# A fast-matmul MLP kernel on one core: every steady step issued from one list, row half by row half, with the side strip's matmuls kept among the main ones

## The chip, the cores and the metric

One core of a Trainium2 chip. The time is device microseconds of one launch. A profile of one execution comes beside it: what each engine (TensorE PE and its weight loader PEld, VectorE DVE, ScalarE ACT, GpSimd POOL, SyncE SP) did and when.

## What is computed

Two blocks in a row, all in fp32: a light convolution over 7 positions with weights softmaxed per head (8 heads, 192 channels, 8 sequences of 4096), then an MLP with a sigmoid GELU (192 to 2048 to 192).

```python
w = np.exp(weight - weight.max(-1, keepdims=True)); w /= w.sum(-1, keepdims=True) + 1e-9
x_pad = np.concatenate([np.zeros((B, 6, D)), x], axis=1)
conv[b, s, h, :] = sum(w[h, k] * x_pad[b, s + k, h, :] for k in range(7))
h = conv.reshape(B * S, D) @ moe_w_in            # (32768, 192) @ (192, 2048)
g = h * (1.0 / (1.0 + np.exp(-1.702 * h)))
out = g @ moe_w_out                              # (32768, 2048) @ (2048, 192)
```

## The kernel before

Both matmuls are done by a fast scheme in blocks: sums of blocks of the inputs and of the weights are multiplied, and the products are added up again, so that fewer products are needed. The work is cut into 32 steps (`N_BIG`), each of 512 tokens from each half of the batch. Step 0 and most of step 1 are the opening, which also prepares the weights; step 31 is the last. A step has two stages on TensorE.

**First stage (products).** For each of two halves `v` of the hidden dimension there are 20 products (`TERMS`). `product1` (L598) issues one as two matmuls, for the row halves h0 and h1: 64 x 128 weights, 512 columns, one in the upper 64 rows of the array and one in the lower, so that two run at a time. The results gather in four pairs of PSUM banks, `slot0` to `slot3` (`sums` is the last); `slot20` is bank pair 2 for h0, `slot21` the same for h1. A product on top of an earlier one in its bank waits until whoever reads the earlier one has done so: DVE adds and subtracts them (`sum2`, L639), ACT copies them out to SBUF rooms (`copy2`, L633, with its sign turned L635), ACT's GELUs read PSUM by halves (L615) or a room at once (L620). The names in the lists: `a0` to `a8` are bank pairs, `k0` to `k10` places in the rooms, and two k names may share one room (k8 and k4 do). POOL meanwhile adds the convolution's taps for the next step (L501, 12 additions a step) and sums of its blocks (`vsum`, L355 and L357), SP copies these sums to the other row half (`cross`, L526); DVE makes the first sums of GELU blocks ("early g", five of them, one by an accumulating DMA on POOL's queue, L831: `(8, 0, "acc")`, spot 8 gets spot 0 added).

**Second stage.** 20 forms times sums of GELU blocks go to PSUM as 78 main steps, each of three matmuls of 128 x 32 weights and 256 columns in the column strips 0, 1 and 2 of the array (L855), and seven more forms go as 78 side matmuls to strip 3 (also L855). DVE makes the sums of GELU blocks just ahead (`sum`, 128 x 1024), adds up the results (`join`), and transposes them (`turn`, L771); ACT copies side results out (L880) and seeds banks (L884), and computes taps of later steps (L483); SP stores (L782).

**What sets the order.** All engines take their instructions in the order in which the program lists them. For the first stage that is `ORDER` (line 646 on), whose items always issue both row halves, h0 and then h1; for the second stage `PLAN` (790 on). There a `("go", n)` issues n times one main step and the next side matmul, so the sequence is always main c0, c1, c2, side. What is done for later steps comes from queues (`next_tap`, `next_add`, `next_sum`, `cross_piece`): a list's item says only that the next one of its queue is issued here. The last step uses the same lists, with what belongs to later steps left out.

The banks of the second stage are the three that come free, in the order in which they come free: `bx`, `bs`, `by`. Mains write their h0 banks in the order `bs, bx, by` and the sides write the h1 banks, `sides = (bx[1], bs[1], by[1])`: a column of the form goes to the first, the next to the second, and so on.

```python
def go(n):
    for _ in range(n):
        w, t = now["steps"].pop(0)
        for c in range(NC):
            one_matmul(chunk(now["to"], c), w[:, chunk_cols(c)], t, now["first"], not now["steps"])
        now["first"] = False
        d, ws, ts, st, to = side.pop(0)
        one_matmul(d, ws, ts, st, to is not False)
```

## Time and profile before

| what | value |
| --- | --- |
| median of 3 runs | 2262.71 us (2261.76 to 2263.1) |
| the profiled execution | 2262.78 us, its span 2261.1 us |
| granted TensorE clock | 1.00 |
| a steady step, first stage / second stage | 35.42 / 33.94 us |
| the last step | 35.07 / 33.88 us |
| end of the last matmul to the end of the span | 2255.57 to 2261.1 us |

The span is what the profile covers; the execution's own time is 1.7 us more. Lines with "chain" come from the profile's way back from the last instruction: at each step to what released it. In a row of the timeline stand start, duration, engine, line, operation, output and input by the program's names, shapes, the number of instructions in the row and, in brackets, the idle time before it with what ended it. An fp32 matmul leaves two records on PE and two weight loads on PEld.

### The profile page before, as it was taken

Reading aid. Unit: us, or ns where it says so; the run is one execution under the profiler, and the core shown is the slowest. Engines: PE = TensorE matmul, PEld = TensorE weight load, DVE = VectorE, ACT = ScalarE, POOL = GpSimd, SP = SyncE. Lnnn points to the kernel's source line nnn. Section 1 sums busy time; section 2 is a strip of 40 time slices with the busy share of each in tenths; the row PEclk is TensorE's granted clock in tenths of the full one; section 3 lists DMA queues with packets and bytes.
Section 4 is the critical chain, followed back from the end, with each engine's and each line's share of the span. In section 5 each row is a group of like instructions: output and inputs, shape, how many; then the busy total and the mean of one; then the engine's idle time right before and its main releaser. Section 6 shows DMA issues by size and latency. Waiting matters only on the chain.

```text
span 2261.1 us, 62136 instructions
## 1 busy us (share of the span) xinstructions
PE 2248.2 (99%) x24966; PEld 1552.0 (69%) x24966; DVE 1985.3 (88%) x2970; ACT 1707.7 (76%) x3233; POOL 1063.9 (47%) x1098
## 2 busy tenths in 40 slices
PE   9999999999999999999999999999999999999999
PEld 5366567766777766777667776667776677766775
DVE  8998888988889888889888898888988888988888
ACT  8677877777777778777787777787777877777754
POOL 1545544455543555444555445554355544455510
PEclk9999999999999999999999999999999999999999
DMA  8986657766667666576565776666866657765543
GB/s 198 174 158 133 125 114 150 143 128 127 121 131 159 128 128 126 111 160 140 125 132 114 141 152 128 129 124 118 163 134 128 124 114 151 144 127 103 104 92 71
DMA packets 275679, 298.05 MB, mean 132 GB/s; under 512 B 119104, under 2 KB 203328, under 8 KB 275392
## 3 DMA queue, kind: packets, MB, share of 16 engines
q0 software_dynamic: 57648, 150.69, 37.0%
q1 hardware_dynamic: 216096, 142.99, 27.8%
q8 instruction: 198, 3.24, 0.6%
q14 instruction: 89, 0.73, 0.1%
q10 hardware_dynamic: 1648, 0.39, 0.1%
HBM read 53.15 MB, written 25.17 MB: 35 GB/s over the span
## 4 chain that ended last, share of the span: by engine, by line
PE 96%; DVE 2%; ACT 1%; issue 1%; DMA 1%; POOL 0%; DVEq 0%; ACTq 0%; POOLq 0%; SPq 0%
PE slot L598 49%; PE slot L855 45%; PE slot L1120 1%; DVE g L357 1%; DMA g<-osbs 0%; PE slot L1115 0%; DVE room L357 0%; ACT g L615 0%; PE slot L946 0%; DVE room L639 0%; ACT w_form L483 0%; DMA xin<-in_x_dram 0%; DVE slot L639 0%; DVE room L355 0%; DVE osbs L771 0%
## 5 line engine op out<-in xcount | busy, mean ns | idle before, releaser
L598 PE MATMUL slot<-conv_t,w_in_s 64*128 64x512 f32 x5152 | 1147.4, 594 | 3.3 <-ACT room L633 1.5
L598 PEld LDWEIGHTS slot<-conv_t,w_in_s 64*128 64x128 f32 x5152 | 663.3, 186 | 474.6 <-issue 312.1
L855 PE MATMUL slot<-g,w_form 128*32 128x256 f32 x9672 | 894.2, 379 | 0.7 <-DVE room L357 0.7
L855 PEld LDWEIGHTS slot<-g,w_form 128*32 128x32 f32 x9672 | 575.6, 110 | 128.9 <-DVE room L357 2.1
L501 POOL TENSOR_TENSOR conv_t<-conv_t,g 128x512 f32<-128x512 f32 x354 | 449.0, 1275 | 88.4 <-ACT g L483 65.4
L855 PE MATMUL slot<-g,w_out_s 128*32 128x256 f32 x5952 | 467.5, 379 | 1.3 <-DVE g L357 0.8
L357 DVE TENSOR_TENSOR g<-g 128x1024 f32<-128x1024 f32 x372 | 450.4, 1224 | 8.0 <-DMA g<-osbs 1.0
L880 ACT COPY room<-slot 32x256 f32<-32x256 f32 x651 | 237.2, 364 | 289.8 <-PE slot L855 281.5
L639 DVE TENSOR_TENSOR room<-slot,room 128x512 f32<-128x512 f32 x620 | 383.6, 679 | 67.8 <-PE slot L598 67.8
L633 ACT COPY room<-slot 128x512 f32<-128x512 f32 x620 | 337.7, 595 | 77.7 <-PE slot L598 61.7
L483 ACT ACTIVATE g<-xt,cw 128x512 f32<-128x512 f32 x534 | 353.9, 715 | 3.7
L620 ACT ACTIVATE g<-room 128x1024 f32<-128x1024 f32 x248 | 265.7, 1071 | 79.0 <-DVE room L639 49.3
L615 ACT ACTIVATE g<-slot 128x512 f32<-128x512 f32 x528 | 282.5, 610 | 51.9 <-PE slot L598 32.8
L831 POOL DMA_DIRECT2D g<-g x124 | 128.1, 1038 | 355.0 <-PE slot L855 330.8
L639 DVE TENSOR_TENSOR slot<-slot,room 128x512 f32<-128x512 f32 x372 | 239.7, 689 | 53.8 <-PE slot L598 52.2
L855 PEld LDWEIGHTS slot<-g,w_out_s 128*32 128x32 f32 x5952 | 239.7, 110 | 43.2 <-DVE room L639 23.3
L355 POOL TENSOR_TENSOR conv_t<-conv_t 128x256 f32<-128x256 f32 x210 | 179.3, 860 | 129.2 <-PE slot L598 119.6
L855 PE MATMUL slot<-osbs,w_form 128*32 128x256 f32 x2232 | 229.5, 379 | 0.0
L506 POOL DMA_DIRECT2D g<-g x120 | 105.9, 883 | 238.1 <-ACT g L483 99.4
L855 PEld LDWEIGHTS slot<-osbs,w_form 128*32 128x32 f32 x2232 | 132.5, 110 | 23.6
L639 DVE TENSOR_TENSOR slot<-room,slot 128x512 f32<-128x512 f32 x124 | 79.8, 687 | 41.8 <-PE slot L598 41.8
L855 PE MATMUL slot<-room,w_form 128*32 128x256 f32 x1488 | 112.9, 379 | 0.0
(166 smaller groups left out, 1662.6 us busy)
## 6 DMA issues: line engine op xcount, KB each, us to landing
g<-g POOLq DMA_DIRECT2D x124, 512.0 KB, 6.5
xin<-in_x_dram SPq DMA_DIRECT2D x240, 180.0 KB, 4.2
conv_t<-conv_t SPq DMA_DIRECT2D x186, 192.0 KB, 5.4
g<-g POOLq DMA_DIRECT2D x120, 256.0 KB, 5.4
conv_t<-conv_t SPq DMA_DIRECT2D x186, 128.0 KB, 2.9
out_dram<-osbs SPq DMA_DIRECT2D x186, 128.0 KB, 2.7
g<-room POOLq DMA_DIRECT2D x31, 512.0 KB, 5.1
conv_t<-g POOLq DMA_DIRECT2D x60, 256.0 KB, 5.4
```

The costliest lines, as they stand in the source:

```text
L355: eng.tensor_add(v(dst), v(a), v(b))
L357: eng.tensor_sub(v(dst), v(a), v(b))
L483: act.mul(home, conv_src(big, c, k), cw[:, c, k : k + 1])
L501: nc.gpsimd.tensor_add(dst, dst, home)
L598: nc.tensor.matmul(slot[h], w_in_s[halves[h], a, v * P : (v + 1) * P], src, start=first, stop=True, skip_group_check=True,)
L615: act.activation(dst[:, :, h, :], src[h].rearrange("p (o t) -> p o t", o=2), AF.Gelu_apprx_sigmoid, scale=float(sign),)
L620: act.activation(dst.rearrange("p o h t -> p h o t"), src.rearrange("p h (o t) -> p h o t", o=2), AF.Gelu_apprx_sigmoid, scale=float(sign),)
L633: act.copy(bank(dst, h), bank(src, h))
L639: op(*(bank(t, h) for t in (dst, a, b)))
L831: nc.gpsimd.dma_start(out=spot(dst), in_=spot(a), accum_op=ALU.add)
L855: nc.tensor.matmul(dst, w, t, start=first, stop=last, skip_group_check=True)
L880: act.copy(to, d)
```

## The change

The two lists and the queues are replaced by one list, `STEP` (L543 on), that names every instruction of a steady step (steps 2 to 30) one by one: products, sums, copies and GELUs of a single row half, a main step `("m", i)`, a side matmul `("s", i)`, each tap, tap addition, sum and crossing copy by its own number. The last step has a list of its own, `LAST` (L1161 on). The opening is written out in the same way. The multiset of instructions on each engine stays as it was; one store of the last step moves from ACT's DMA queue to SP's.

```diff
-    ORDER = [
-        (0, "prod", 6, "a8"), (0, "sum", "k0", "a8", "-", "k8"), (0, "prod", 2, "a3"), (0, "copy", "k4", "a3", 1),
...
-    PLAN = [
-        ("side", 13, 16, "k0"), ("main", 1, 5, "p2", 1), ("vsum",), ("go", 2), ("sum", 14, 14, "-", 18), ("go", 1),
...
+    STEP = [
+        ("add", 1, 2, 5), ("tap", 1, 1, 6), ("add", 1, 1, 6), ("prod", 0, 6, "a8", 0),
+        ("sum", 0, "k0", "a8", "-", "k8", 0), ("prod", 0, 6, "a8", 1), ("sum", 0, "k0", "a8", "-", "k8", 1),
...
+        ("begin", 0), ("s", 0), ("s", 1), ("m", 0), ("m", 1), ("s", 4), ("m", 3), ("s", 7), ("m", 5),
...
+        ("s", 68), ("turn", 0, 0, 1, "k1"), ("turn", 0, 1, 1, "k2"), ("t", 20), ("m", 74),
...
-        mains, sides = (bs[0], bx[0], by[0]), (bx[1], bs[1], by[1])
+        mains, sides = (bs[0], bx[0], by[0]), (by[1], bx[1], bs[1])
...
+    def main_part(i):
+        dst, w, t, first, last = now["todo"][i]
+        for c in range(NC):
+            one_matmul(chunk(dst, c), w[:, chunk_cols(c)], t, first, last)
+
+    def side_part(i):
+        d, w, t, first, to = now["aside"][i]
+        one_matmul(d, w, t, first, to is not False)
...
+    opening()
+    for big in range(2, N_BIG - 1):
+        run(STEP, big)
...
+    run(LAST, N_BIG - 1)
```

Products are now issued by L483, second-stage matmuls by L744, copies and seeds by L537, turned copies by L539, GELUs by L500, side copies by L779, taps by L446, tap additions by L450, accumulating DMAs by L533, sums and joins by L343 and L345. In the second stage two or three sides, or two or three main steps, may now follow each other directly; counted along the list, the number of sides issued is at no point more than two ahead of the main steps, nor more than one behind.

**Start of a steady step's first stage.** PE, before: the products 6, 2, 12, 16 and 14, whole.

```order
L598 MATMUL slot00_67<-conv_t_78,w_in_s_79 128x512
L598 MATMUL slot01_68<-conv_t_78,w_in_s_79 128x512
L598 MATMUL slot20_71<-conv_t_78,w_in_s_79 128x512
L598 MATMUL slot21_72<-conv_t_78,w_in_s_79 128x512
L598 MATMUL slot30_73<-conv_t_78,w_in_s_79 128x512
L598 MATMUL slot31_74<-conv_t_78,w_in_s_79 128x512
L598 MATMUL slot10_69<-conv_t_78,w_in_s_79 128x512
L598 MATMUL slot11_70<-conv_t_78,w_in_s_79 128x512
```

PE, after, at the same place: 6 (both halves), 12 of h0, 2 of h1, 12 of h1, 2 of h0, 16 of h1 and of h0.

```order
L483 MATMUL slot00_67<-conv_t_78,w_in_s_79 128x512
L483 MATMUL slot01_68<-conv_t_78,w_in_s_79 128x512
L483 MATMUL slot30_73<-conv_t_78,w_in_s_79 128x512
L483 MATMUL slot21_72<-conv_t_78,w_in_s_79 128x512
L483 MATMUL slot31_74<-conv_t_78,w_in_s_79 128x512
L483 MATMUL slot20_71<-conv_t_78,w_in_s_79 128x512
L483 MATMUL slot11_70<-conv_t_78,w_in_s_79 128x512
L483 MATMUL slot10_69<-conv_t_78,w_in_s_79 128x512
```

Products 2 and 12 have changed places in h0 only. Then come 9 of h0 and 14 of h1; before, 14 of h0 and h1, and 9 behind it. ACT's first copies, before, behind the last side copy of the step before:

```order
L880 COPY room_76<-slot11_70 32x256
L483 ACTIVATE g_75<-xt_2189,cw_143 128x512 x3
L633 COPY room_76<-slot20_71 128x512
L633 COPY room_76<-slot21_72 128x512
L483 ACTIVATE g_75<-xt_2189,cw_143 128x512
L633 COPY room_76<-slot10_69 128x512
L633 COPY room_76<-slot11_70 128x512
```

and after:

```order
L779 COPY room_76<-slot11_70 32x256
L446 ACTIVATE g_75<-xt_2186,cw_143 128x512 x3
L537 COPY room_76<-slot21_72 128x512
L537 COPY room_76<-slot20_71 128x512
L537 COPY room_76<-slot10_69 128x512
L537 COPY room_76<-slot11_70 128x512
```

The copy of product 2 into k4 takes h1 first, and no tap stands between it and the copy of product 16 into k1.

**Start of the second stage.** PE, before: the last product, and main steps and sides in turn (a row x3 is one main step, a row with an h1 slot one side).

```order
L598 MATMUL slot31_74<-conv_t_78,w_in_s_79 128x512
L855 MATMUL slot00_67<-g_75,w_out_s_80 32x256 x3
L855 MATMUL slot01_68<-g_75,w_form_81 32x256
L855 MATMUL slot00_67<-g_75,w_out_s_80 32x256 x3
L855 MATMUL slot01_68<-g_75,w_form_81 32x256
```

PE, after:

```order
L483 MATMUL slot30_73<-conv_t_78,w_in_s_79 128x512
L744 MATMUL slot11_70<-g_75,w_form_81 32x256 x2
L744 MATMUL slot00_67<-g_75,w_out_s_80 32x256 x6
L744 MATMUL slot01_68<-g_75,w_form_81 32x256
L744 MATMUL slot00_67<-g_75,w_out_s_80 32x256 x3
L744 MATMUL slot01_68<-g_75,w_form_81 32x256
L744 MATMUL slot00_67<-g_75,w_form_81 32x256 x6
```

Two sides come first, in another bank (slot11, the tile whose last reader is a GELU, instead of slot01, which a DVE sum reads last), then two main steps in a row.

**POOL ahead of the second stage.** Before, from the run of tap additions (L501) on; L831 is the accumulating DMA into spot 8:

```order
L501 TENSOR_TENSOR conv_t_78<-conv_t_78,g_75 128x512 x12
L355 TENSOR_TENSOR conv_t_78<-conv_t_78 128x256
L357 TENSOR_TENSOR conv_t_78<-conv_t_78 128x256
L355 TENSOR_TENSOR conv_t_78<-conv_t_78 128x256
L357 TENSOR_TENSOR conv_t_78<-conv_t_78 128x256
L355 TENSOR_TENSOR conv_t_78<-conv_t_78 128x256 x3
L831 DMA g_75<-osbs_77 128x1024
L357 TENSOR_TENSOR conv_t_78<-conv_t_78 128x256 x2
L355 TENSOR_TENSOR conv_t_78<-conv_t_78 128x256 x2
```

After:

```order
L450 TENSOR_TENSOR conv_t_78<-conv_t_78,g_75 128x512 x11
L343 TENSOR_TENSOR conv_t_78<-conv_t_78 128x256
L345 TENSOR_TENSOR conv_t_78<-conv_t_78 128x256
L450 TENSOR_TENSOR conv_t_78<-conv_t_78,g_75 128x512
L343 TENSOR_TENSOR conv_t_78<-conv_t_78 128x256
L345 TENSOR_TENSOR conv_t_78<-conv_t_78 128x256
L343 TENSOR_TENSOR conv_t_78<-conv_t_78 128x256 x3
L345 TENSOR_TENSOR conv_t_78<-conv_t_78 128x256
L343 TENSOR_TENSOR conv_t_78<-conv_t_78 128x256
L533 DMA g_75<-osbs_77 128x1024
```

One tap addition now stands among the sums, and the accumulating DMA is behind nine of them instead of seven.

More of the change, by code (lines that the diff above doesn't have):

```diff
@@ L452, in tap_home @@
     def tap_home(big, c, k):
+        if k == 0:
+            return own(big)[:, 2 * c : 2 * c + 2, :]
         if big == 1:
@@ L828, in sum_g @@
[L828 to L858 removed]
+    def sum_g(dst, a, op, b):
+        add_up(spot, dst, a, op, b)
@@ new lines, in begin, with value, one_matmul @@
+                copies.append((chunk(value(to), c), dst))
+    def value(name):
+        i = int(name[1:])
+        return now["mains"][i // 2][0:n3, i % 2 * T : (i % 2 + 1) * T] if name[0] == "p" else kept(i)
+    def one_matmul(dst, w, t, first, last):
+        nc.tensor.matmul(dst, w, t, start=first, stop=last, skip_group_check=True)
+    def main_part(i):
+        dst, w, t, first, last = now["todo"][i]
+        for c in range(NC):
+            one_matmul(chunk(dst, c), w[:, chunk_cols(c)], t, first, last)
@@ L1131, in first_step, with main0, side0 @@
         }
+        aside(
+            (sums[0], sums[1], c11),
+            (listed(s1, t1, (0,)), None, True), (listed(s1, t1, (1,)), p5, False), (p3[:6], q12, False),
+        )
+        def main0(name, what, i, first, stop):
+            w, t = steps[what][i]
+            for c in range(NC):
+                one_matmul(chunk(banks[name], c), w[:, chunk_cols(c)], t, bool(first), bool(stop))
+        def side0(i):
+            dst, w, t, start, to = side[i]
+            one_matmul(dst, w, t, start, to is not False)
@@ L1195, in first_step @@
-            cross=cross_piece,
-            turn=lambda m, n, src: turn(m, n, blocks(value[src]), js),
-            store=store,
-            trees=end_taps,
-            do=lambda what, *item: do(1 + what // 2, what % 2, halves_1[what], *item),
-            fill=lambda *item: fill(1, *item),
-        )
-        free.extend((slots[2], sums, slots[0], slots[1]))
-        for item in OPENING:
-            ops[item[0]](*item[1:])
-        assert not side and not w_left
-    def begin(big):
-        todo.extend(prepare(big))
-        ready.extend(prepare_taps(big))
```

720 lines of the change are left out of this document (270 added, 450 removed), and 386 rows, old and new, of tables (LAST, MAINS, OPENING, ORDER).

## The prediction, as it was put on record

> **What bounds the kernel now.** I read the page first: busy times, the slices, the shares of the chain.
>
> ```profile
> span 2261.1 us, 62136 instructions
> PE 2248.2 (99%) x24966; PEld 1552.0 (69%) x24966; DVE 1985.3 (88%) x2970; ACT 1707.7 (76%) x3233; POOL 1063.9 (47%) x1098
> PEclk9999999999999999999999999999999999999999
> PE 96%; DVE 2%; ACT 1%; issue 1%; DMA 1%; POOL 0%; DVEq 0%; ACTq 0%; POOLq 0%; SPq 0%
> ```
>
> TensorE holds 96% of the chain at a full clock throughout, so only its own time counts: the sum of its matmuls, and the gaps among them. "99% busy" does not say that there are no gaps: two matmuls run at once in the first stage and four in the second, and PE counts as busy while one of them runs. So next comes the chain of waits in order of time (start, duration, what), around two steps in the middle and at the end.
>
> ```profile
> 1007.58 35.42 PE slot L598 x157
> 1042.99 33.94 PE slot L855 x624
> 1076.93 35.41 PE slot L598 x157
> ...
> 2186.62 35.07 PE slot L598 x153
> ```
>
> ```profile
> 2221.70 33.88 PE slot L855 x624
> 2255.57 0.41 DVE room L355
> ```
>
> A step is 35.42 us of first-stage products (L598) and 33.94 us of second stage (L855), 69.36 us in all: from 1007.58 to 2186.62 there are 17 steps, and 1179.04 / 17 = 69.36. Steps 2 to 30 are alike (29 of them); the last begins at 2186.62. Windows over the two stages give each engine's load (engines in the order PE, PEld, DVE, ACT, POOL, each busy us and count, then clock, DMA share, GB/s):
>
> ```profile
> 1007.50:1042.90 35.40, 35.40 (x161) 20.68 (x160) 29.84 (x45) 28.71 (x50) 25.02 (x24) 1.00 0.54 112
> 1042.90:1076.90 34.00, 34.00 (x627) 28.72 (x626) 31.07 (x47) 24.85 (x52) 9.40 (x11) 1.00 0.79 154
> ```
>
> No other engine fills a stage; DVE comes nearest, with 31.07 of 34.00. So the order of work can win only the gaps inside TensorE's two stages. Their size comes from the weight loads of the first stage. An fp32 matmul leaves two records, that is two passes; a step's 80 products (20 terms, two halves of the hidden dimension, two row halves of the array) are 160 records, and with both row halves at work 80 passes.
>
> ```profile
> 1007.50 0.30 PEld L598 LDWEIGHTS slot<-conv_t,w_in_s 64*128 64x128 f32 x4 [0.41 <-issue]
> 1008.04 0.19 PEld L598 LDWEIGHTS slot<-conv_t,w_in_s 64*128 64x128 f32 x2 [0.24 <-ACT room L633]
> ...
> 1010.78 6.89 PEld L598 LDWEIGHTS slot<-conv_t,w_in_s 64*128 64x128 f32 x33 [0.40 <-ACT room L633]
> ...
> 1018.82 0.29 PEld L598 LDWEIGHTS slot<-conv_t,w_in_s 64*128 64x128 f32 x2 [0.39 <-POOL conv_t L501]
> ...
> 1025.79 0.26 PEld L598 LDWEIGHTS slot<-conv_t,w_in_s 64*128 64x128 f32 x2 [0.17 <-issue]
> ...
> 1035.23 0.34 PEld L598 LDWEIGHTS slot<-conv_t,w_in_s 64*128 64x128 f32 x2 [0.17 <-issue]
> ...
> 1036.12 0.29 PEld L598 LDWEIGHTS slot<-conv_t,w_in_s 64*128 64x128 f32 x2 [0.20 <-ACT slot L635]
> ...
> 1041.87 0.29 PEld L598 LDWEIGHTS slot<-conv_t,w_in_s 64*128 64x128 f32 x2 [0.30 <-DVE slot L639]
> ```
>
> Between 1025.79 and 1035.23 lie 22 passes without a stall: 9.44 / 22 = 0.429 us a pass. 80 passes are 34.33 us, so of the 35.42 us 1.09 us are gaps. About 0.2 of them belong to every start of the stage: 1007.50 to 1008.04 is 0.54, or 0.11 over the pitch, and the change of array shape is about 0.09 (below). The remaining **0.89 us a step** are stalls in which one row half waits: for ACT's copy into a room at 1010.78, for POOL's tap sums, by name, at 1018.82, for ACT's activations that empty a bank at 1036.12, for a DVE sum at 1041.87. The list of waits of the weight loads tells the same for the whole run (total us, times, longest):
>
> ```profile
> PEld slot L598 <- ACT room L633: 26.6, 89, 1.6
> PEld slot L855 <- DVE room L639: 23.3, 30, 1.3
> PEld slot L598 <- DVE slot L639: 19.9, 71, 1.9
> PEld slot L598 <- ACT slot L635: 18.1, 92, 0.3
> PEld slot L598 <- POOL conv_t L501: 10.9, 28, 0.4
> ```
>
> These are idle times of the loader, part of which belongs to the ordinary pitch (0.17 to 0.24 before a load that waited only for its turn), so they name the stalls and don't size them.
>
> For the second stage I read its two edges in the order of time:
>
> ```profile
> 1041.73 2.47 DVE L639 TENSOR_TENSOR room<-slot,room 128x512 f32<-128x512 f32 x4
> ...
> 1042.92 0.42 PE L855 MATMUL slot<-g,w_out_s 128*32 128x256 f32 x3
> ...
> 1043.11 0.38 PE L855 MATMUL slot<-g,w_form 128*32 128x256 f32 x1
> ...
> 1043.16 0.39 PE L855 MATMUL slot<-g,w_out_s 128*32 128x256 f32 x3
> ```
>
> ```profile
> 1076.40 0.39 PE L855 MATMUL slot<-g,w_out_s 128*32 128x256 f32 x3
> ...
> 1076.56 0.38 PE L855 MATMUL slot<-g,w_form 128*32 128x256 f32 x1
> ...
> 1076.87 5.41 PE L598 MATMUL slot<-conv_t,w_in_s 64*128 64x512 f32 x23
> ```
>
> The three main strips start at 1042.92; the first side matmul, in the fourth strip, starts 0.19 later, since its bank is read by the second of DVE's four sums from 1041.73 (two of 0.62 us end at 1042.97). The lag never closes: the side's last pass starts at 1076.56, 0.16 after the mains' last. From 1043.16 to 1076.40 there are 154 passes: 33.24 / 154 = 0.2158. 78 matmuls a strip are 156 passes, 33.67 us; of the stage's 33.94 the other 0.27 are that 0.16 and the edge: 1076.56 + 0.216 = 1076.78 to the first product at 1076.87, 0.09.
>
> **The change part by part.** The instructions stay the same; no duration or count on TensorE changes, and the floor is 34.33 + 33.67 a step. What can change are the gaps.
>
> First stage. The new order issues the row halves one by one, so that a half that is ready doesn't wait behind its partner, and it turns their order round where the second one was late. The stall at 1010.78 is such a place:
>
> ```profile
> 1009.10 1.25 DVE L639 TENSOR_TENSOR room<-slot,room 128x512 f32<-128x512 f32 x2
> ...
> 1010.14 1.07 ACT L633 COPY room<-slot 128x512 f32<-128x512 f32 x2
> ```
>
> Product 14 goes to the bank that the copy into k4 empties, and k4 takes the room of k8, which DVE's two sums (k0, h0 and h1) read until 1010.35. The copies go h0, h1; the second ends at 1011.21, while 14 is the fifth of its half and due four pairs (3.43 us) after 1007.58, at 1011.01. Now h1 is copied first: from 1010.4 to 1011.0, just in time or 0.1 late, and h0's 14 comes one pair later. The stalls at 1018.82 and 1036.12 are one place in the two halves of the hidden dimension: product 19 goes to the bank that ACT's negating copy (L635) takes from product 10, with one product (17) between them. POOL, named at 1018.82, writes nothing that product 19 reads, and its run of twelve additions goes on there; ACT's copies fit:
>
> ```profile
> 1018.17 1.07 ACT L635 ACTIVATE slot<-slot 128x512 f32<-128x512 f32 x2 [0.25 <-PE slot L598]
> ```
>
> h0 is copied at 1018.7 and h1 at 1019.24, and h0's load starts at 1018.82, h1's behind it. In the new order h0 has two products between, h1 one, but h0's 10 comes a pair ahead of h1's, so that h1's copy no longer waits behind h0's: 0.55 for a copy against 0.86 for a product. The other stalls are treated in the same way. I went through the new order with the pitch of 0.429 and the trace's durations (0.6 for a sum or copy of one half, as in the rows above): most places keep 0.05 to 0.3 us, and only product 14 stays up to 0.1 short. Where less than 0.1 is left a weight load may come late. Bounds: nothing left (0), or all left (0.89). I take **0.25**, nearer to nothing, because 14's 0.1 and two late loads of under 0.1 are what I can point to. The first stage becomes 34.33 + 0.20 + 0.25 = 34.78, 0.64 less.
>
> Second stage. The first side goes to the bank of the tile that a GELU has emptied about two products earlier, and both edges are ordered side, side, main and main, side, main. The 0.16 goes, the 0.09 stays: 33.79, 0.15 less, bounded by 0 and 0.18. What else could stop the mains there? DVE's big sums, one run from 1.3 us after the stage's start:
>
> ```profile
> 1044.18 4.76 DVE L357 TENSOR_TENSOR g<-g 128x1024 f32<-128x1024 f32 x4
> ```
>
> 4.76 / 4 is 1.19 each. Counting these sums in their new order against 0.43 us a main step, the tightest main has about 0.6 us to spare, nearly what the old order has. DVE hides this; with that cover gone each us of a late sum is a us of the step.
>
> Moved DMAs. The accumulating transfer 8←0 leaves POOL's queue behind the sums of the next step's blocks:
>
> ```profile
> 1037.21 0.87 POOL L831 DMA_DIRECT2D g<-osbs  x1 [1.63 <-ACT room L633]
> ```
>
> ```profile
> g<-osbs POOLq DMA_DIRECT2D x30, 512.0 KB, 7.2
> ```
>
> Issued 5.7 us before the second stage and landing after 7.2, it came 1.5 us into it. Behind the sums I put it at 4.3 before, landing 2.9 in; DVE's second sum, which waits for it, could start at 2.5. That is 0.4 late, and the main that needs the result has about 0.9: cost nothing, at worst (all the sums on POOL slower by half) 1 us. SP's crossing copies are issued 17 us or more before their products, one store of the last step moves from ACT's queue to SP's: nothing, both under the matmuls, or behind them by under 1 us once.
>
> Last step: 35.07 before; 39 pairs are 78 passes, 33.47, with 0.20 and 0.25 33.92: 1.15 less, and 0.15 of its second stage: 1.30. The end behind the last matmul is unchanged. The opening keeps its order.
>
> Sum: (0.64 + 0.15) x 29 = 22.9, with 1.3: 24.2. The profiled execution took 2262.78 (span 2261.1 plus 1.7 around it), the median of the runs is 2262.71. **2262.8 − 24.2 = 2238.6.** With no stall left it is (0.89 + 0.16) x 29 + 1.6 = 32 less, 2231; with all of the first stage's stalls kept only 4.5 less, 2258.
>
> **The rivals.**
>
> *The stalls move.* Every engine has the same work in less time: DVE 60.9 us (29.84 + 31.07) in 68.6 instead of 69.4, 89%. If the waits that go uncover others, half of the 24.2 or nothing remains: 2250 to 2262. For it speaks that many new margins are below 0.3 us, while one sum takes 0.6; against it that before's stalls come from clear queueing, not from load.
>
> *The strips start strictly in order of issue* (slower). Before, the second stage always issues main, main, main, side: each strip gets one in turn. The new one has runs of two or three sides, or of two main steps, so a strip has two neighbours in the queue. If a matmul can't start before all those issued ahead of it have, the second of two sides holds back the main behind it. Counted through the new list this is 87 rounds instead of 78 (last step: 85), each 2 x 0.2158 = 0.4316: 3.9 us a step, against the 0.79 won: (3.88 − 0.79) x 29 + 3.0 − 1.3 = 91, **2354**. It decides from the first round lost: two a step eat the gain. Against it: the side's first pass at 1043.11 starts before the mains' second passes at 1043.16, though the mains were issued first: strips hold their own place at least from pass to pass. No row of before shows two neighbours for one strip. The Trainium skill ("TensorE: Matmul & The Clock Gate", section "The mechanism") states that matmuls start and end strictly in program order, without reordering; by that rule this rival would hold, and the order of 1043.11 and 1043.16 goes against the rule at the level of passes.
>
> *The transfer 8←0 comes too late* (slower). DVE's queue is strictly in turn here, so its second big sum holds all behind it. From 0.9 us of lateness each us costs 29: at 1.9 late 2239 + 29 = 2268. For it: its place behind nine sums instead of seven; against it: POOL is at 9.40 of 34.00 in the second stage and its sums are short.
>
> **How the numbers follow.** Forecast 0.69; the stalls move 0.16, of which 0.06 within 0.2% (4.5 us, about what a measurement of this kernel can tell from no change); strict order 0.09; late transfer 0.06. Faster 0.69 + 0.10 = 0.79, same 0.06, slower 0.15. The range goes from 2229 (no stall left, and the 1.3 us by which the runs differ) to 2264 (all stalls moved, and that spread again); left out are the two slower rivals and some hundredths.
>
> **What would show it.** Right: the chain shows about 34.8 us of products and 33.8 of second stage a step; the loader's waits for ACT's rooms and slots shrink, and the one put down to POOL with them; the wait of the second stage's first load for DVE is gone; the side strip starts with the mains and ends with them. Wrong: a second stage above 35 us with all strips empty at times (strict order), DVE idle behind the accumulating transfer, or first-stage products still over 35.2 with new names in the list of waits.

## The result, and the profile after

The changed kernel takes 2278.3 us (median of 4 runs) against 2262.9 before: ratio 1.0075, 95% interval 1.0054 to 1.0095. It is slower by 0.75% where 1.1% faster was forecast. Its page and the waits of its weight loads (total us, times, longest):

```profile
span 2277.0 us, 61602 instructions
PE 2249.1 (99%) x24966; PEld 1463.1 (64%) x24966; DVE 2006.9 (88%) x2970; ACT 1721.3 (76%) x3233; POOL 1081.6 (48%) x1098
```

```profile
PEld slot L483 <- ACT room L537: 41.3, 122, 1.6
PEld slot L744 <- ACT g L500: 23.9, 31, 1.2
...
PEld slot L483 <- POOL conv_t L450: 16.6, 18, 2.4
```

The totals look like those of before; PE is again "99% busy". One line stands out: POOL's additions (L450) are waited for only 18 times, but up to 2.4 us long, where before 28 waits were at most 0.4. The chain of this profile breaks off 94 us before the end, so I took the stages from the starts of their first matmuls. Windows over the first stages of two steps and one second stage (columns as in the prediction):

```profile
1011.62:1048.40 36.78, 35.20 (x163) 20.81 (x160) 31.65 (x46) 28.55 (x49) 25.14 (x23) 1.00 0.47 98
1153.45:1188.39 34.94, 34.94 (x164) 21.12 (x160) 29.81 (x46) 28.66 (x49) 24.95 (x23) 1.00 0.49 103
1188.39:1222.80 34.41, 34.41 (x627) 24.81 (x625) 31.17 (x46) 25.33 (x53) 10.07 (x12) 1.00 0.82 163
```

The steady steps are no longer alike. 15 of the 29 have a first stage of 34.94 to 35.06 us, 12 one of 36.2 to 36.8 (two lie between). All second stages but the last of the 29 take 34.40. So there are three changes, in sums over the 29 steps, worked out from these starts:

| | before | after | difference |
| --- | --- | --- | --- |
| first stages | 1028.5 | 1032.7 | +4.2 |
| second stages | 985.1 | 997.8 | +12.7 |
| last step and tail (to the end of the span) | 74.5 | 73.8 | -0.7 |

Had the 12 long first stages been like the short ones, the first stages would have gained 14; the long ones cost 18.

**A long step and a short one.** First the long step that begins at 1011.62. The view is the timeline (POOL's additions from a window of their own, so that the first one stands alone):

```profile
1012.07 0.86 POOL L454 DMA_DIRECT2D conv_t<-g  x1 [3.02 <-issue]
1012.64 1.60 POOL L450 TENSOR_TENSOR conv_t<-conv_t,g 128x512 f32<-128x512 f32 x1
```

```profile
1012.24 2.29 DVE L343 TENSOR_TENSOR room<-room 96x256 f32<-96x256 f32 x1
...
1015.14 1.24 DVE L345 TENSOR_TENSOR room<-slot,room 128x512 f32<-128x512 f32 x2
...
1016.47 2.05 ACT L537 COPY room<-slot 128x512 f32<-128x512 f32 x4 [2.41 <-DVE room L345]
1017.14 1.56 PE L483 MATMUL slot<-conv_t,w_in_s 64*128 64x512 f32 x6 [1.58 <-POOL conv_t L450]
```

and the short one that begins at 1153.45:

```profile
1154.08 0.42 DVE L343 TENSOR_TENSOR room<-room 96x256 f32<-96x256 f32 x1
...
1155.11 1.25 DVE L345 TENSOR_TENSOR room<-slot,room 128x512 f32<-128x512 f32 x2
...
1155.76 0.86 POOL L454 DMA_DIRECT2D conv_t<-g  x1 [5.40 <-issue]
1156.33 1.59 POOL L450 TENSOR_TENSOR conv_t<-conv_t,g 128x512 f32<-128x512 f32 x1
```

The reader is to follow one DVE instruction, the last join of the step before (`k8`), 0.62 us behind the first product in both. It takes 0.42 us in the short step. In the long one it takes 2.29: it ends at 1014.53, just behind POOL's first tap addition (1012.64 + 1.60 = 1014.24). Everything behind it in DVE's queue comes 1.9 us late, first the two k0 sums (which, with one input in PSUM, take their usual 0.62 each although POOL's second addition runs beside them, 1014.13 to 1015.66); ACT's copies wait for these (2.41), and product 14 for the copy. The profile puts TensorE's wait down to POOL's L450, which is not what product 14 waits for; but here the name points to the culprit, two steps back.

What decides between long and short is when POOL starts. Its queue holds the last accumulating transfer of the taps (L454), which waits until the one before has landed, and then the additions. Over the 29 steps L454 was issued between 0.1 us before the first product and 2.3 after it. In all 12 long steps it came at 0.48 or earlier, in the others at 0.60 or later. The first addition's row starts about 0.57 behind it: in the long steps at 1.04 or earlier, ahead of the join's ordinary end (1.05 us into the step), in the others at 1.17 or later, when the join is over. By the rows the addition need not be first: in five of the long steps, the one shown among them, it starts 0.2 to 0.4 us behind the join, and yet the join ends last. Rows on POOL are rough, so which of the two really began first there is not shown. Before, the same transfer varied as much, but in 28 of the 29 steps the first addition came 4.4 us into the step, since it needs a tap that ACT makes there (in the first one later still).

**The second stage.** Its start is as forecast; side and main steps begin together, in the timeline of PE at 1048.40:

```profile
1048.40 0.40 PE L744 MATMUL slot<-g,w_form 128*32 128x256 f32 x1
1048.41 0.42 PE L744 MATMUL slot<-g,w_out_s 128*32 128x256 f32 x3
1048.64 0.38 PE L744 MATMUL slot<-g,w_form 128*32 128x256 f32 x1
1048.66 0.39 PE L744 MATMUL slot<-g,w_out_s 128*32 128x256 f32 x3
1048.86 0.38 PE L744 MATMUL slot<-g,w_form 128*32 128x256 f32 x1
```

The order of issue is side, side, main. Each matmul has two passes, so the second side begins at 1048.86, in its strip's third pass, and the main step issued behind it has started both its passes by then (1048.41 and 1048.66). Strips are not held to the order of issue. The 0.46 us by which the stage grew (34.40 against 33.94) are lost later, and with them what the new start saved. From strip to strip I took the starts of passes and looked for intervals over 0.2158: in the step from 1188.39 the mains lose 0.05 at the start, 0.3 at the 49th main step (21 us into the stage), 0.13 to 0.18 at the 60th and 0.05 at the 63rd. ACT is the one waited for at the 49th and at the 60th:

```profile
1208.97 0.35 ACT L779 COPY room<-slot 32x256 f32<-32x256 f32 x1
...
1209.37 0.22 PEld L744 LDWEIGHTS slot<-g,w_form 128*32 128x32 f32 x6 [0.40 <-ACT room L779]
```

```profile
1212.33 0.37 ACT L779 COPY room<-slot 32x256 f32<-32x256 f32 x1 [0.21 <-PE slot L744]
1212.72 0.73 ACT L446 ACTIVATE g<-xt,cw 128x512 f32<-128x512 f32 x1
1213.47 0.58 ACT L537 COPY room<-slot 128x512 f32<-128x512 f32 x1
1213.96 0.38 ACT L537 COPY slot<-room 96x256 f32<-96x256 f32 x1
```

At the 49th a side copy ends at 1209.32 and the loads go on at 1209.37. At the 60th a side copy waits for TensorE, then come a tap, a copy and the seed into p1; the seed ends at 1214.34 and the 60th main step, which adds to p1, starts at 1214.386; with the pitch and the 0.05 of the start alone it was due at 1188.41 + 59 x 0.4316 + 0.05 = 1213.92, so it is 0.47 late. In the step from 1048.40, which lost its time at other places ahead, it starts as long after the stage's start (25.98 us against 25.99). That fits second stages that all have the same length.

### The profile page after: what moved, and what is told of

It reads as the page before. It is cut to its first block, busy times and chain, and to the rows that moved or that the text cites. A ratio compares the mean times of both kernels' runs of the same rounds, so it can differ in the third digit from the quotient of the medians.

```text
span 2277.0 us, 61602 instructions
## 1 busy us (share of the span) xinstructions
PE 2249.1 (99%) x24966; PEld 1463.1 (64%) x24966; DVE 2006.9 (88%) x2970; ACT 1721.3 (76%) x3233; POOL 1081.6 (48%) x1098
## 5 line engine op out<-in xcount | busy, mean ns | idle before, releaser
L483 PE MATMUL slot<-conv_t,w_in_s 64*128 64x512 f32 x5152 | 1135.8, 593 | 18.9 <-POOL conv_t L450 10.0
L483 PEld LDWEIGHTS slot<-conv_t,w_in_s 64*128 64x128 f32 x5152 | 673.7, 186 | 468.1 <-issue 257.7
L744 PE MATMUL slot<-g,w_form 128*32 128x256 f32 x9672 | 939.1, 380 | 0.6 <-DVE room L345 0.6
L744 PEld LDWEIGHTS slot<-g,w_form 128*32 128x32 f32 x9672 | 546.3, 110 | 239.7 <-ACT g L500 22.7
L537 ACT COPY room<-slot 128x512 f32<-128x512 f32 x806 | 409.4, 539 | 291.2 <-PE slot L744 143.6
L744 PE MATMUL slot<-g,w_out_s 128*32 128x256 f32 (+1 forms) x6048 | 505.4, 383 | 1.7 <-DVE g L345 0.8
L450 POOL TENSOR_TENSOR conv_t<-conv_t,g 128x512 f32<-128x512 f32 x354 | 456.9, 1319 | 16.9 <-ACT g L446 2.7
L345 DVE TENSOR_TENSOR g<-g 128x1024 f32<-128x1024 f32 x372 | 447.2, 1222 | 3.3
L345 DVE TENSOR_TENSOR room<-slot,room 128x512 f32<-128x512 f32 x620 | 362.2, 626 | 12.1 <-PE slot L483 4.8
L446 ACT ACTIVATE g<-xt,cw 128x512 f32<-128x512 f32 x534 | 359.6, 716 | 3.3
L779 ACT COPY room<-slot 32x256 f32<-32x256 f32 x651 | 234.4, 364 | 134.4 <-PE slot L744 122.3
L500 ACT ACTIVATE g<-slot 128x512 f32<-128x512 f32 x528 | 294.4, 604 | 41.9 <-PE slot L483 25.7
L533 POOL DMA_DIRECT2D g<-g x124 | 107.6, 870 | 385.9 <-PE slot L744 171.5
L500 ACT ACTIVATE g<-room 128x1024 f32<-128x1024 f32 x248 | 264.8, 1068 | 30.4 <-DVE room L345 17.8
L343 POOL TENSOR_TENSOR conv_t<-conv_t 128x256 f32<-128x256 f32 x210 | 203.5, 975 | 169.1 <-PE slot L483 161.7
L744 PE MATMUL slot<-osbs,w_form 128*32 128x256 f32 x2232 | 258.3, 379 | 0.0
L744 PEld LDWEIGHTS slot<-g,w_out_s 128*32 128x32 f32 x6048 | 226.1, 109 | 22.1 <-DVE slot L343 6.0
L454 POOL DMA_DIRECT2D g<-g x120 | 104.8, 873 | 244.0 <-ACT g L446 168.8
L343 DVE TENSOR_TENSOR slot<-slot,room 128x512 f32<-128x512 f32 (+1 forms) x155 | 93.7, 641 | 95.9 <-ACT room L537 52.2
L343 DVE TENSOR_TENSOR room<-slot,room 128x512 f32<-128x512 f32 (+1 forms) x248 | 136.4, 551 | 46.0 <-PE slot L483 30.8
L345 DVE TENSOR_TENSOR slot<-slot,room 128x512 f32<-128x512 f32 x248 | 163.2, 692 | 12.6 <-PE slot L483 8.8
L744 PEld LDWEIGHTS slot<-osbs,w_form 128*32 128x32 f32 x2232 | 121.8, 110 | 48.2
```

Of the source, the lines that this page charges most:

```text
L343: eng.tensor_add(v(dst), v(a), v(b))
L345: eng.tensor_sub(v(dst), v(a), v(b))
L446: act.mul(tap_home(big, c, k), conv_src(big, c, k), cw[:, c, k : k + 1])
L450: nc.gpsimd.tensor_add(tap_home(big, c, 0), tap_home(big, c, 0), tap_home(big, c, k))
L454: nc.gpsimd.dma_start(out=tap_home(big, c, a), in_=tap_home(big, c, b), accum_op=ALU.add)
L483: nc.tensor.matmul(slot[h], w_in_s[halves[h], a, v * P : (v + 1) * P], src, start=first, stop=True, skip_group_check=True,)
```

## Experiments

Times are medians of several runs each; the kernel before took 2262.9 to 2263.2 beside them. "First" and "second" are the lengths of a steady step's stages.

**1. The first addition behind its tap.** Theory: POOL's addition holds DVE's join. Rival: the transfers that land irregularly are the cause themselves.

```diff
-        ("add", 1, 2, 5), ("tap", 1, 1, 6), ("add", 1, 1, 6), ("prod", 0, 6, "a8", 0),
+        ("tap", 1, 1, 6), ("add", 1, 1, 6), ("add", 1, 2, 5), ("prod", 0, 6, "a8", 0),
```

> The changed kernel, but each step's first tap addition on POOL is one that needs a tap which ACT makes 2.5 us after the step's start (the two additions at the head of the list change places, the tap ahead of both). Theory (POOL's addition, when it starts ahead of DVE's last join of the step, 0.63 us after the products begin, holds that join up until it ends): the join takes 0.42 us in all 29 steps instead of 1.7 to 2.3 in 12 of them, all first stages are about 34.95 us, and the 19 us that the long ones cost go: 2278 to about 2259. Rival (the long first stages come from the transfers that land irregularly, and the addition only follows them): 12 or so first stages of over 36 us stay, 2278 within 3. The second stage stays at 34.40 by both.

Measured 2260.2 (ratio to before 0.9988, 0.9978 to 0.9997): 18 us less than the changed kernel. The join takes 0.42 in 28 of the 29 steps (0.38 in the first), no first stage is over 36, 27 of 29 are below 35.1. The transfers still land as irregularly as before. A step with an early one:

```profile
1005.01 0.86 POOL L454 DMA_DIRECT2D conv_t<-g  x1 [3.02 <-issue]
1005.19 0.42 DVE L343 TENSOR_TENSOR room<-room 96x256 f32<-96x256 f32 x1
...
1007.10 2.49 POOL L450 TENSOR_TENSOR conv_t<-conv_t,g 128x512 f32<-128x512 f32 x2 [1.23 <-ACT g L446]
```

The transfer is issued 0.18 us ahead of the join, as in a long step, and the join is not delayed: it is the addition that holds it, not the issue of a DMA on POOL.

**2. The same in the kernel before.** Three of its additions go ahead of the last tap transfer (a new item of `PLAN` that calls `next_add` three times).

```diff
-        ("turn", 1, 1, 1, "k2"), ("tree",), ("go", 1),
+        ("turn", 1, 1, 1, "k2"), ("adds",), ("tree",), ("go", 1),
```

> The kernel before, with three of the twelve tap additions on POOL issued ahead of the last accumulating transfer of the taps, so that they run from about 2.4 us before the products start to 1.5 us after; no other instruction moves. Theory (a DVE sum of two SBUF tiles waits for a running POOL addition): DVE's last join, 0.81 us after the products' start, ends about 0.7 us later, the first two sums of the step with it, and the first stage grows by 0.4 to 0.7 us: 2263 + 12 to 20 = 2275 to 2283. Rival (POOL and DVE don't touch, and the additions only come earlier): 2263 within 3, or faster.

Measured 2272.6 (1.0043, 1.0026 to 1.0060), 9.5 us slower, in the direction of the theory and below its range. POOL, then DVE, around a step that begins at 731.08:

```profile
728.69 4.32 POOL L501 TENSOR_TENSOR conv_t<-conv_t,g 128x512 f32<-128x512 f32 x3
...
731.89 1.40 DVE L355 TENSOR_TENSOR room<-room 96x256 f32<-96x256 f32 x1
```

The join, 0.38 in the kernel before, takes 1.40 and ends at 733.29, behind the third addition (733.01). The size is smaller than expected since it doesn't happen to the full in every step. In 18 of the 29 the third addition's row starts 0.1 us or more before the join's (0.81 us into the step), and the join takes 1.07 to 1.45. In the others POOL came later, so that the join met only the end of the second addition, or nothing; six joins take their 0.38. The third addition can then be the one that waits, as in the step that begins at 940.65:

```profile
941.44 1.55 POOL L501 TENSOR_TENSOR conv_t<-conv_t,g 128x512 f32<-128x512 f32 x1
...
941.46 0.38 DVE L355 TENSOR_TENSOR room<-room 96x256 f32<-96x256 f32 x1
```

The addition takes 1.55 instead of 1.27, and the join, which starts 0.02 behind it by the rows, is not held. So each holds up the other, and here the one that comes clearly first runs through.

**3 and 4. ACT's order in the second stage.** The seed of p1 goes ahead of the side copy, tap and copy shown above, and another side copy (t9, which the queue at the 49th main step waits for) ahead of a tap; alone, and with experiment 1.

```diff
-        ("m", 54), ("t", 14), ("s", 56), ("m", 48), ("tap", 2, 0, 6),
+        ("m", 54), ("seed", "p1", "k1", 1), ("t", 14), ("s", 56), ("m", 48), ("tap", 2, 0, 6),
...
-        ("gsum", 6, 14, "+", 6), ("seed", "p1", "k1", 1), ("m", 50),
+        ("gsum", 6, 14, "+", 6), ("m", 50),
...
-        ("t", 10), ("s", 37), ("tap", 2, 0, 4), ("m", 35), ("t", 9), ("m", 46)
+        ("t", 10), ("s", 37), ("t", 9), ("tap", 2, 0, 4), ("m", 35), ("m", 46)
```

> The changed kernel, with two places of ACT's order in the second stage mended: the seed of p1 goes ahead of a tap, a copy and the side copy that waits for TensorE, and one side copy into k1 goes ahead of a tap. Theory (main steps wait 0.3 and 0.4 us for ACT at these two places in every step, one of them directly and one behind a side matmul that waits): the second stage falls from 34.40 to between 33.9 and 34.1, 29 x 0.3 to 0.5 = 9 to 14 us less, 2278 to 2264 to 2269; the long first stages stay. Rival (the 0.46 us come from strips that hold each other up where sides or mains follow each other, not from ACT): 34.40 stays, 2278 within 3.

> Both edits of the two kernels ahead of this one. If both causes are as the theories say, they add: all first stages 34.95, second stage 33.9 to 34.1, and 2278 - 19 - (9 to 14) = 2245 to 2250, faster than the kernel before (2262.9) by 0.6 to 0.8%. If the time comes out over 2259, one of the two has been replaced by another wait.

Measured 2271.3 (1.0036, 1.0023 to 1.0049) and 2255.6 (0.9967, 0.9954 to 0.9980). The two causes add (18 and 5 to 7 us), and the kernel is now faster than the one before; but the second stage fell only from 34.40 to 34.25. The two waits are gone and two others show. In the kernel with both edits, at the 55th and the 63rd main step:

```profile
646.58 0.37 ACT L779 COPY room<-slot 32x256 f32<-32x256 f32 x1 [0.22 <-PE slot L744]
...
646.82 0.15 PEld L744 LDWEIGHTS slot<-g,w_out_s 128*32 128x32 f32 x6
```

```profile
649.65 0.37 ACT L537 COPY room<-slot 96x256 f32<-96x256 f32 x1
...
650.05 0.43 DVE L343 TENSOR_TENSOR slot<-slot,room 96x256 f32<-96x256 f32 x1 [1.63 <-ACT room L537]
650.54 0.15 PEld L744 LDWEIGHTS slot<-g,w_out_s 128*32 128x32 f32 x6 [0.16 <-DVE slot L343]
```

The 55th main step, issued behind three sides in a row, comes 0.12 late; the 63rd waits for a DVE join that waited for a seed (0.23 late).

**5. Two more places of ACT.**

```diff
-        ("copy", 2, "k8", "a3", 1, 1), ("tap", 2, 0, 1), ("tap", 2, 0, 0), ("t", 11), ("t", 8), ("t", 10),
+        ("t", 8), ("copy", 2, "k8", "a3", 1, 1), ("tap", 2, 0, 1), ("tap", 2, 0, 0), ("t", 11), ("t", 10),
```

(and the seed of k5 ahead of the tap in front of it).

> The kernel with both edits (2255.6 us), and two more places of ACT's order in the second stage mended: the side copy t8 goes ahead of a copy and two taps, and the seed of k5 ahead of a tap. Theory (the second stage's 34.25 us hold 0.23 us in which main steps wait for a DVE join that waits for the seed of k5, and 0.12 us in which the fourth strip, late by a wait for t8, holds up the mains issued behind three sides in a row): the second stage falls to 33.9 to 34.0, 29 x 0.25 to 0.35 = 7 to 10 us less: 2245 to 2249. Rival (the wait only moves on, to the next sum or copy): 34.15 to 34.25, 2252 to 2256.

Measured 2303.4 (1.0178, 1.0163 to 1.0193): the theory's repair made it 48 us worse, second stage 35.92. The row shows why:

```profile
722.00 0.36 ACT L779 COPY room<-slot 32x256 f32<-32x256 f32 x1 [1.11 <-PE slot L744]
```

ACT reached t8 before TensorE had released it and stood for 1.11 us, with a copy, two taps and three side copies behind it; the sides that need these came late (the fourth strip by 1.24 us) and all strips with them: the mains lose 0.75 at the 47th main step. Another 0.55 goes at the 72nd, where a side waits for a later side copy; which of the two edits put that copy behind is not told apart. "Earlier in the queue" is no gain if the instruction then waits at its head. The 0.23 at the seed of k5 also stayed: with the tap out of the way the seed waited for TensorE instead.

**6. DVE's last transposition later**, on top of experiment 5: `("turn", 1, 1, 0, "k8")` and its store go behind the next step's first four sums.

> The kernel ahead of this one, with DVE's last transposition of a step (k8) and the store of its half moved behind the next step's first four sums. Theory (of the first stage's 34.95 us 0.2 are a stall of products 14 and 9 for DVE's first sums, which stand behind the step's last joins and transpositions): these sums come 0.35 us earlier and the first stage falls to 34.7 to 34.8: 4 to 7 us less than the kernel ahead of this one. Rival (that stall is ACT's, whose taps stand ahead of the copies): 34.95 stays, within 2 us of the kernel ahead.

Measured 2303.7, the same as experiment 5; the first stage stays at 34.97 against 34.97. The sums start only 0.15 us earlier, since they then wait for product 6 itself, and the rest of the stall turns up at the neighbouring pair and at the thirteenth. Neither theory nor rival holds as put. I took the stall for a loop of product, sum, copy and product that is as long as the work between, but that is not shown, and a late engine has a part in it. In the short step at 1153.45 the second row half of product 6 starts 0.25 us behind the first, since its bank waits for an ACT side copy of the step before: the copy ends at 1153.65, the load starts at 1153.71. In experiment 9 the same list of the first stage follows a longer second stage, that half starts only 0.09 late, and the first stage takes 34.80.

**7. Side banks as before.** On the kernel of experiment 4:

```diff
-        mains, sides = (bs[0], bx[0], by[0]), (by[1], bx[1], bs[1])
+        mains, sides = (bs[0], bx[0], by[0]), (bx[1], bs[1], by[1])
```

> The kernel with both edits (2255.6 us), with the side banks of the second stage in the order of the kernel before (bx, bs, by). The first side then writes a bank that a DVE sum reads last, as before. Theory (in the kernel before the fourth strip starts 0.16 us late and stays late for that reason; here the first two sides are issued ahead of the mains and hold these up as well): the second stage grows by 0.1 to 0.3, 2258 to 2264. Rival (the bank order is of no account, the lag of 0.16 came from the place of the first side in the order): 2255.6 within 2.

Measured 2272.7 (1.0043, 1.0028 to 1.0057), 17 us more. The second stage grew by 0.30 to 34.55, as expected, and the first by 0.29 to 35.24, which I had not expected. A stage is counted up to the first matmul of the next, and that is where the 0.29 lie: the last passes of the products start 34.40 us into the stage, against 34.42 in experiment 4, but the first side comes 0.3 later.

```profile
696.04 0.68 DVE L345 TENSOR_TENSOR room<-slot,room 128x512 f32<-128x512 f32 x1
...
696.79 0.11 PEld L744 LDWEIGHTS slot<-g,w_form 128*32 128x32 f32 x1 [1.05 <-ACT g L500]
...
697.25 0.68 DVE L345 TENSOR_TENSOR room<-slot,room 128x512 f32<-128x512 f32 x1
...
697.99 0.11 PEld L744 LDWEIGHTS slot<-g,w_form 128*32 128x32 f32 x1 [0.57 <-DVE room L345]
```

The stage's first load starts just behind the second of DVE's last four sums, which ends at 696.72 and reads the bank that the first side now writes (the profile names ACT, whose GELU was over at 696.34). Later another side waits for the last of these sums, which ends at 697.93, and the strips, mains too, start again together at 697.99.

**8. TensorE's own order**: a main step of form 12 goes ahead of the 63rd, and the sides 49 and 51 change places.

> The kernel with both edits (2255.6 us), with TensorE's own order mended instead of ACT's: one main step that needs nothing late (the third of form 12, into p3) goes ahead of the main step into p4 that waits for a DVE join, and two sides change places so that the one which waits for the side copy t8 comes later. Theory (0.23 us of the second stage are a loop: a main step ends, ACT seeds k5, DVE joins p2, the next main step into p4 starts, with only three main steps between; 0.12 us come from the side that waits for t8): the second stage falls from 34.25 to 33.9 to 34.05, 6 to 10 us less: 2246 to 2250. Rival (the wait moves on to the next join): 34.15 to 34.25, 2252 to 2256.

Measured 2266.4 (1.0015, 1.0005 to 1.0024), 11 us worse, second stage 34.64. Both halves of the theory fell. The main step put ahead writes p3, in one bank with p2, and waited as long as the one it replaced (0.23); and side 49 waits for a later side copy than side 51: its strip came 0.54 late, and the mains at the 55th main step 0.4, where they had lost 0.12.

**9. Sides and mains in turn.** Strictly in turn throughout, other instructions at their places; main steps and sides then pass seeds, copies and sums that they should follow, so the sums in PSUM are others than the reference's:

> The kernel with both edits (2255.6 us), with the same main steps and sides in the same orders, but strictly in turn (side, main, side, main), all other instructions at their places among them. The rival of the prediction (a strip's second neighbour holds back what is issued behind it) gives a second stage shorter by up to 3.9 us; a weak form of it (only three in a row, and only by what the strip is late) 0.1 to 0.2, 3 to 6 us less. Theory (strips take their turns independently, as the loads of neighbours in the trace show): 34.25 stays within 0.1, or grows where a main step now stands ahead of its sum; 2255.6 within 3.

Measured 2372.4, second stage 38.45. No strip gains; at several places in each stage one instruction waits for ACT (141.5 us in all, 175 times, in the list of waits), and all four strips stop until it goes on, 0.2 to 1.1 us a place. That shows the other half of the rule: strips run ahead of each other, but an instruction that waits for another engine stops all that are behind it.

**10 and 11. Short runs.** Sides and mains in turn only where nothing stands between them, on the kernel of experiment 4, and on that of experiment 1 with ACT's order left alone. A piece of the list:

```diff
-        ("s", 62), ("s", 63), ("s", 65), ("m", 51), ("s", 58), ("m", 61), ("s", 59), ("m", 60),
+        ("s", 62), ("s", 63), ("m", 51), ("s", 65), ("m", 61), ("s", 58), ("m", 60), ("s", 59),
```

> The kernel with both edits (2255.6 us), with sides and main steps put in turn wherever no other instruction stands between them: runs of three go from 11 to none, runs of two from 32 to 18, everything else keeps its place. By the strict order of the prediction's rival the second stage would need 80 rounds instead of 87, 3.0 us a step less than now (2168). Theory (strips take their turns independently as long as a strip has no more than one matmul waiting; a third in a row holds up what is behind it only by what its strip is late): at most the 0.12 us at one such place go, 34.1 to 34.3, 2251 to 2257.

> The kernel with the tap addition behind its tap (2260.2 us, second stage 34.40), with only the sides and main steps put in turn as in the short-runs kernel, and ACT's order left as the changed kernel has it. Theory A (the runs and ACT's two places are two causes that add: 0.30 and 0.15 us a step): second stage 34.10, 2251 to 2252.5. Theory B (the runs are the one cause; the waits for ACT only show where a strip had fallen behind): 33.95, 2246 to 2248. Theory C (without ACT's order mended the two places hold the stage as before): 34.4, 2259 to 2261.

Measured 2246.9 (0.9929, 0.9914 to 0.9944) and 2252.4 (0.9953, 0.9936 to 0.9970). The first is the fastest kernel of this study, 0.7% faster than the one before. It went below the theory's range, though far from the strict rule's 2168. Its windows (a first and a second stage):

```profile
654.95:689.89 34.94, 34.94 (x163) 21.10 (x160) 29.82 (x46) 28.66 (x49) 24.88 (x23) 1.00 0.50 103
689.89:723.85 33.96, 33.96 (x627) 23.69 (x625) 31.18 (x46) 25.18 (x53) 10.07 (x12) 1.00 0.84 165
```

The second stage is 33.95, 0.30 less: not only the 0.12 behind three sides, also most of the 0.23 at the 63rd main step (0.07 is left) and the fourth strip's wait for t8 went. Experiment 11, where ACT's two places stay, has 34.13: theory A. So of the 0.46 us about 0.30 are the runs (34.25 to 33.95, or 34.40 to 34.13) and about 0.15 ACT's order (34.40 to 34.25, or 34.13 to 33.95).

**12. Copies by halves in the kernel before.** The copies into k4 and a5 take h1 first, the products as they were.

> The kernel before, with the two row halves of the copies into k4 and a5 in the other order (h1 first, as the changed kernel has it for k4), the products as they were. Theory (the copies' order alone only moves the stall to the other half, since product 14 and product 19 come with both halves together; the gain needs the products' order by halves too): the first stage stays at 35.42 within 0.1, 2263 within 3. Rival (the second half's stall goes and the first half has room): 35.1, 2254.

Measured 2317.9 (1.0241, 1.0224 to 1.0258), first stage 37.06 instead of 35.42. The theory (the stall only moves) was too mild:

```profile
820.43 1.07 ACT L633 COPY room<-slot 128x512 f32<-128x512 f32 x2 [0.31 <-PE slot L598]
...
821.55 4.99 PE L598 MATMUL slot<-conv_t,w_in_s 64*128 64x512 f32 x22 [0.33 <-ACT room L633]
```

The copies end at 821.0 (h1) and 821.5 (h0). Product 14's h0 is issued first, waits for the later copy and keeps h1's, whose bank is free, behind it: both halves start at 821.55, 0.5 us late. Before, only h1 was 0.2 to 0.3 late. The stage grew by more than this, 1.64: later products lose as well (0.3 to 0.6 us at four more places), and the waits there were not followed.

## Why the prediction was wrong

- **The floor and what bounds the kernel** held: the passes kept their pitch (0.429 and 0.2158), and the time moved with the gaps.
- **First stage, 34.78.** The mechanism was right where steps were undisturbed, the gain too large: 34.94 without collisions, 0.47 less than before instead of 0.64. The residual is 0.41, not 0.25. In the short step at 1153.45 one row half loses 0.20 at product 14 and 0.19 at its 25th product. These late loads cost about twice what I counted: the second pass of a product that started late is late by another 0.1, as the second pass of each stage is. The other half loses 0.25 at product 6, to the ACT side copy named under experiment 6, a wait that the prediction did not have.
- **The first stage's slack, the step that failed most.** "Most places keep 0.05 to 0.3 us" rested on durations of before, where the last join takes 0.38 us in all steps. I read the twelve additions' row only as POOL's load and let them start earlier at no cost. Of the edit's own terms I asked what queues behind a moved instruction, not what else uses what it uses. Experiments 1 and 2 show it: 18 us, more than the whole gain of the first stage. The rule was there to be read: the Trainium skill ("SBUF — State Buffer", section "Who interferes with whom") says that a DVE `tensor_tensor` with both inputs in SBUF contends with GpSimd's reads, and that the contention is an exclusive lock in which the order of issue decides who blocks. The traces agree on the lock: 2.29 us instead of 0.42, to the end of the addition, while the issue of a DMA on POOL does not do it. On the order experiment 2 agrees; in the long steps of the changed kernel the rows leave it open, since the join's row can start 0.4 us ahead and still end last.
- **Second stage, 33.79.** Failed: 34.40. The step was "DVE hides this", with 0.6 us to spare. It counted DVE's big sums alone, and the first four of these were on time; I did not count ACT's copies and seeds, nor that a side waiting for one of them stops the mains behind it. Experiments 3, 4, 10 and 11 give the parts, about 0.15 for ACT's order and 0.30 for the runs. The edge was right: the 0.16 went, and experiment 7 shows what the old banks would cost.
- **The rival of the moving stalls** (2250 to 2262) is near what was left once the collisions were gone: experiment 1 gives 2260.2, and what the first stage gained there the second lost. The collisions themselves no rival had.
- **The rival of strict order**, 2354, did not come: mains start while sides issued ahead of them wait for their strip (1048.41). By the rule of the Trainium skill that I weighed ("TensorE: Matmul & The Clock Gate", section "The mechanism") they could not. The row that I held against it beforehand, a side at 1043.11 ahead of the mains' second passes at 1043.16, was weaker than it looked: it compares passes, and the matmuls themselves had started in order. What is true in the rule is weaker: runs of neighbours cost 0.30 us a step, not 3.9, and waits for other engines do stop everything behind. Which limit in TensorE's queue makes the runs cost 0.30 stays open.
- **The rival of the late transfer 8←0** did not come: DVE's first four big sums still run without a gap.

```profile
1189.79 4.76 DVE L345 TENSOR_TENSOR g<-g 128x1024 f32<-128x1024 f32 x4
```

- **Last step**: 0.7 less instead of 1.3. Its first stage is 34.21 (0.86 less), but its second loses 0.5 as the steady ones do; the end behind the last matmul, which I had put as unchanged, is 0.3 shorter.

## What to carry to other kernels

An instruction that is moved takes along what it shares with other engines: before letting a GpSimd elementwise operation start earlier, look which DVE operations with two SBUF inputs it will now meet, above all when its start hangs on a transfer whose landing varies by microseconds; here a tie to an ACT operation 2.5 us into the step was worth 18 us. A stall that differs from step to step in a kernel of equal steps is looked for by sorting the steps, long against short, and comparing one of each. In a tight order the slack must be counted round whole loops (matmul, copy, seed, matmul), and an in-order queue is served worst by what waits at its head.

## What the runs showed of the hardware

- A DVE sum of two SBUF tiles (96 x 256, 0.38 to 0.42 us) that meets a POOL addition of SBUF tiles ends 0.3 us behind that addition: 2.29 us in the changed kernel, 1.40 in experiment 2. Where the sum is let through, the addition waits: 1.55 us instead of 1.27 in experiment 2. A DVE sum with one input in PSUM is not held (0.62 us beside a running addition).
- The wait for one and the same accumulating transfer, in the same place of different steps, varied by microseconds: POOL stood 3.0 us ahead of the next one in the steps from 1011.62 and 1004.56, 5.4 in that from 1153.45.
- On TensorE four column strips keep their own pace (a pass each 0.2158 us) with sides up to three in a row: in the step from 1048.40 a main step starts 0.45 us ahead of a side issued before it. An instruction that waits for another engine stops what is issued behind it, in experiment 9 all four strips, 0.2 to 1.1 us at each of seven places in a stage.
